# Raw weight slices issued one by one inside the table of orders, on one core

## The chip, the cores and the metric

The kernel runs on one core of a Trainium2 chip. The metric is the device time of one execution in microseconds; the kernel before takes 1088.55 us (median of 3 runs, 1088.54 to 1089.48). The engines are called as in the profile: PE is TensorE's matmul stream, PEld its weight loads, DVE VectorE, ACT ScalarE, POOL GpSimd, SP SyncE. A Q behind the name (ACTq, SPq) marks an instruction that only issues a DMA from that engine's queue.

## The reference

Random-feature attention over 8 batches of 8 heads, 576 tokens, head size 64, 128 features; its output, as a matrix of 4608 tokens by 512, goes through a feed-forward layer of width 2048.

```
def phi(x):                                  # x scaled by 64**-0.25
    proj = einsum('bhsd,md->bhsm', x, omega)
    h = proj - sum(x*x, -1)/2
    h = h - max(h, -1)
    return exp(h) / sqrt(m)
kv  = einsum('bhsm,bhsd->bhmd', phi(k), v);  z = sum(phi(k), axis=2)
num = einsum('bhsm,bhmd->bhsd', phi(q), kv)
den = einsum('bhsm,bhm->bhs', phi(q), z) + 1e-6
x = (num / den) as (tokens, heads*dim)
h = x @ w_in
out = (h - tanh(h)) @ w_out
```

All of it is float32.

## The kernel before

The feed-forward part needs nearly all of TensorE's time. The kernel splits its operands into a hi part (fp32r) and a lo part, and forms each product as hi x hi + hi x lo + lo x hi, three fp32r matmuls in the place of one in float32. Tokens go in 18 chunks of 256, the inner width in 16 slices of 128.

The 16 weight slices arrive as raw 64-bit words, one transfer of 1024 KB each (128 x 1024 words, `raw`), issued from ACT's queue. A slice holds double words of which the kernel makes a float32 by operations on the bits, and then the two fp32r parts. These are the steps of a decoder `d0` to `df`, each a token of the table:

- `is`: issue the raw transfer (ACTq, L619).
- `b` (ACT, L627): the high words to the working buffer `a`; it is the first step that needs the raw slice in place.
- `cl` (POOL, L638; on DVE for d0 and d1): clamp. `v1`, `v2`, `v3` (DVE, L644, L650, L658): shifts and joins of bits.
- `hi` (ACT, L666): the fp32r hi part into the weight's place. `nh` (ACT, L669): minus hi into the lo place.
- `di` (POOL's queue, L672): an accumulating DMA that adds `a` to it, so that the lo part is there when it lands.

The first three batches of keys and the first three chunks of queries are computed by hand-ordered units in float32, at the start. A key unit `kBC` (batch, pair of heads) has `lk` and `lv` (loads on SP's queue, L467, L471), `pj` (projections on PE, L480, L482), `redA`, `redB`, `red5` (minima on DVE, L486, L495), `expA`, `expB`, `exp5` (ACT, L491, L499), `pk0`, `pk1` (products with v on PE, L503, L513), `z` (DVE), `kvf`, `kvwa`, `zb` (ACT copies, L529, L522, L538), `kvwd` (DVE) and `zt` (PE, L533). A query unit `qCC` has `lq` (SP, L551), `pj` (PE, L447), `red` (DVE, L453), `exp` (ACT, L458), `den` (DVE, L562), `nD` and `nA` (DVE and ACT, L569, L574), `pt` (PE transposes, L581), `qt` (ACT, L585), `pn` (PE, L591), `xh` (ACT, L595) and `xl` (DVE). A feed `f0` to `fd` is the feed-forward layer of the first two chunks for one weight slice: `h` (12 matmuls of 512 columns, L373), `th` and `gh` (ACT, L379, L384), `g` and `gl` (DVE, L381, L387), `o` (12 matmuls, L403 to L405). Feed `f0.h` needs all q units of chunks 0 and 1, and each feed needs its own slice's `di` landed.

All these steps stand as 559 tokens in one table, `ORDER`. The program goes through it token by token and every engine and queue gets its instructions in that order, and works through them strictly in it; there is no scheduler in this part. A number behind a step names the buffer or bank it uses (three `kf` and three `v` buffers, two `qf`, eight PSUM banks, three `a` buffers), so a load waits until the buffer's last reader is done. The places of slices 14 and 15 lie over the key buffers, so these two can be issued only when the last key unit has been read. In the table before, the other fourteen `is` tokens are its second to fifteenth.

```
    with tc.manual_schedule():
        for token in ORDER.split():
            name, step_, *slot = token.split(".")
            ...
            units[name][step_](*(int(x) for x in slot))
```

Behind the table come feeds 14 and 15 and then chunks 2 to 17, where a scheduler that goes by modelled times puts the remaining key and query units between the matmuls.

Of the kernel before, what the change touches and what calls it, by code (L numbers as in the profile page):

```python
# [34 lines left out]
TYPES = "dddddddddddddddd"  # L35
BANKS = ("pj0", "pj1", "po0", "po1", "pk", "pt", "h0", "h1")
ORDER = """
k03.lk.0 d0.is d2.is da.is d7.is d4.is d1.is d6.is d3.is dc.is d5.is d9.is d8.is db.is dd.is k01.lk.1 q03.lq.0
k11.lk.2 k03.pj.0.1.2 k01.lv.0 k01.pj.3.4.5 k03.redB k02.lk.0 k03.redA k03.expB.0 k03.red5 q03.pj.6 k01.redB
k12.lk.1 k03.expA.1 k01.red5 q03.red k01.expB.2 k02.lv.1 k01.redA k11.pj.7.1.0 k03.exp5.0 k01.expA.3 k11.lv.2  # L40
k11.redA k01.pk0.4 q03.exp.4 k11.red5 k11.redB k10.lk.2 k11.expA.5 k02.pj.2.3.6 q12.lq.1 k11.exp5.1 k11.expB.6
q13.lq.0 k02.red5 k11.pk0.7 k13.lk.0 k02.redB k02.redA k11.pk1 k02.expB.7 q12.pj.0 k02.expA.3 k11.z k02.pk0.1
k02.exp5.1 q12.red k11.kvf k11.kvwa k02.pk1 k11.kvwd q12.exp.5 k10.lv.2 k11.zt q13.pj.3 k02.z k01.exp5.1
k02.kvf k11.zb k02.zt k12.lv.1 q13.red k01.pk1 k02.zb q12.den q13.exp.6 k13.pj.2.6.0 q01.lq.1 d0.b.0 k01.z
q02.lq.0 q12.nD k03.lv.0 k01.zt q12.nA k13.redB k10.pj.5.7.1 k01.zb k13.redA k13.expB.3 k22.lk.0 k13.red5 d0.cl
q12.pt.3 k13.expA.7 k10.redA q02.pj.6 k23.lk.2 k10.redB k10.expA.2 q01.pj.2 k10.red5 q02.red q00.lq.0
k10.exp5.1 d0.v1 k03.pk0.5 q12.qt.0 q23.lq.1 q02.exp.5 q01.red k03.pk1 d0.v2 k01.kvf q01.exp.1 k10.pk0.1 k03.z
d0.v3 k13.exp5.0 k03.zt k10.expB.0 q12.pn.3 q02.den k10.pk1 k03.zb k00.lv.0 k03.kvf d0.hi q13.den q23.pj.6
k10.kvwa k22.lv.2 k10.kvf d0.nh q00.pj.4 q13.nD k10.z k10.kvwd q13.nA q23.red k12.pj.2.0.7 q11.lq.1 d0.di
d2.b.1 q00.red q21.lq.0 q02.nD k10.zt q23.exp.2 k12.red5 q13.pt.5 k12.redB d2.cl k12.redA q13.qt.1 k12.exp5.1  # L50
q11.pj.6 q03.den k12.expA.0 q13.pn.5 k00.lk.1 k10.zb q11.red q03.nA k12.pk0.7 q03.nD q13.xh q10.lq.1 q01.den
k12.expB.6 q03.pt.2 k12.pk1 q03.qt.0 q01.nD q01.nA q13.xl q03.pn.1 d2.v1 k12.kvwa k12.kvf q00.exp.0 k12.z
k12.kvwd q01.pt.0 d2.v2 k12.zt q21.pj.2 q01.qt.1 k12.zb k23.lv.1 d2.v3 q03.xh q01.pn.5 q02.nA q12.xh q02.pt.4
q03.xl d2.hi q22.lq.0 q12.xl q10.pj.0 q21.red q02.qt.0 k00.pj.7.1.3 q10.red q11.exp.4 q11.den q10.exp.6
q02.pn.4 k00.redB q22.pj.6 q11.nA k00.redA k21.lk.1 q02.xh q01.xh k00.red5 q02.xl k00.expA.1 q01.xl q20.lq.1
q11.nD k00.pk0.0 k00.exp5.1 q22.red d1.b.2 k22.pj.4.5.7 d3.b.0 d1.cl q11.pt.3 d1.v1 k00.expB.5 k22.red5 d3.cl
k22.redB k00.pk1 q11.qt.1 k22.redA k20.lk.0 k22.expB.1 d1.v2 q11.pn.1 k13.lv.0 k00.kvf k22.exp5.1 q20.pj.3
k22.expA.4 k00.z d1.v3 k00.zt k22.pk0.5 q11.xh q20.red k00.zb q22.exp.5 k22.pk1 q11.xl q10.den d1.hi
k21.pj.7.4.0 q10.nD q10.nA q00.den k22.kvwa k13.pk0.1 d1.nh k21.lv.2 k21.redB k13.pk1 q00.nA d1.di k21.red5
k21.expB.4 k21.redA q10.pt.6 k13.z q00.nD k13.zt q10.qt.0 k22.kvwd q00.pt.4 k22.z d3.v1 k13.kvf k13.zb k22.zt  # L60
q00.qt.1 q10.pn.6 q23.den k13.kvwa k21.exp5.1 q00.pn.4 k21.expA.1 k21.pk0.0 q10.xh k13.kvwd q00.xh q23.nD
q23.nA k21.pk1 q00.xl q10.xl k22.zb d3.v2 q21.exp.7 f0.h.7 k20.lv.0 k21.kvwa q21.den d2.nh q20.exp.3 d2.di
k21.z k21.kvwd f1.h.1 d4.b.2 d3.v3 f0.th q21.nD d4.cl d3.hi f0.g q22.den f0.gh q23.pt.4 d3.nh k21.zt
k23.pj.6.5.2 q23.qt.0 f0.gl k21.zb q22.nA q22.nD q23.pn.3 k23.redA f1.th d3.di k23.redB k23.expA.6 q22.pt.7
f1.g k23.pk0.4 q23.xh d4.v1 f1.gh f2.h.0 k23.red5 d6.b.1 f1.gl d4.v2 k23.exp5.0 k23.expB.0 d6.cl d4.v3 q22.qt.1
f0.o f2.th q20.den d4.hi d4.nh f2.g q21.nA f1.o d6.v1 d4.di f2.gh d6.v2 d5.b.0 f2.gl q20.nA d5.cl d6.v3 f3.h.6
q20.nD d6.hi d6.nh f2.o f3.th d6.di f3.g d5.v1 f3.gh d5.v2 d7.b.2 f4.h.7 f3.gl d7.cl d5.v3 d5.hi f3.o f4.th
d5.nh f4.g d7.v1 f4.gh d5.di da.b.1 k23.pk1 f4.gl d7.v2 f4.o k23.kvwa da.cl k23.kvwd k23.z d7.v3 d7.hi k23.zt
q21.pt.0 k23.zb q22.pn.6 d7.nh da.v1 q21.qt.0 f5.h.7 da.v2 d7.di d8.b.0 q22.xh da.v3 d8.cl f6.h.4 da.hi f5.th
da.nh f5.g f5.gh q21.pn.0 da.di f5.gl d8.v1 f7.h.6 f6.th d8.v2 d9.b.2 q21.xh f6.g d9.cl d8.v3 f6.gh f5.o f6.gl  # L70
d8.hi f7.th d8.nh f7.g f6.o d9.v1 f7.gh d8.di dc.b.1 f7.gl d9.v2 dc.cl f7.o d9.v3 d9.hi d9.nh k20.pj.7.0.4
dc.v1 d9.di db.b.0 f8.h.6 k20.redA k20.redB k20.expA.1 db.cl k20.red5 dc.v2 k20.exp5.1 k20.expB.4 k20.pk0.7
dc.v3 f8.th k20.pk1 f8.g dc.hi q20.pt.4 k20.z f8.gh f9.h.0 db.v1 de.is k20.kvwa dd.b.2 f8.gl k20.kvwd db.v2
q20.qt.1 dd.cl df.is dc.nh db.v3 fa.h.6 f9.th f9.g db.hi f9.gh db.nh f8.o f9.gl dc.di dd.v1 fa.th dd.v2 db.di
fa.g f9.o dd.v3 fa.gh fa.gl dd.hi dd.nh fa.o dd.di de.b.1 de.cl k20.zt q20.pn.4 k20.zb df.b.0 fb.h.0 q20.xh
df.cl de.v1 fc.h.6 fb.th de.v2 fb.g de.v3 fb.gh fd.h.7 fb.gl de.hi df.v1 fc.th df.v2 de.nh fb.o fc.g de.di
df.v3 fc.gh fc.gl df.hi fc.o fd.th df.nh fd.g fd.gh df.di fd.gl
"""


# [749 lines left out]
```

## Time and profile before

| | us |
|---|---|
| median of 3 runs | 1088.55 |
| the profiled execution | 1089.21 |
| its span | 1087.2 |
| PE busy (share) | 1046.5 (96%) |
| DVE busy | 804.7 (74%) |
| ACT busy | 677.3 (62%) |
| POOL busy | 278.5 (26%) |
| raw slices: 16 of 1024.0 KB, median to landing | 11.3 |
| `di`: 16 of 512.0 KB, median to landing | 4.8 |
| `k_f`, `v`, `q_f` loads of the table: 288, 320, 128 KB, median to landing | 5.1, 3.6, 3.0 |

The profiled execution is 2.0 us longer than its span, and 0.66 us above the median. Shares of busy time are means over stages that have different limits: PE's 96% holds an opening where it is nearly empty. Matmuls of PE are pipelined and their ends are modelled, so a stretch in which PE counts as busy can hold small gaps; the distance from one start to the next is the better price. Which engine binds is read from a stage's own row.

### The profile page before, as it was taken

To read this page: it belongs to the slowest core of one execution; us is meant where nothing else is said; L and a number is where in the kernel's file an instruction comes from. 1 tells how busy PE (TensorE), PEld (TensorE's weight loads), DVE (VectorE), ACT (ScalarE), POOL (GpSimd) and SP (SyncE) were. 2 spreads that over 40 slices of the span, in tenths; PEclk is the share of its full clock that TensorE was granted. 3 is DMA by queue.
4 is the path that set the end of the run, shared out by engine and by line. 5 is a ranking of instruction groups with operands and counts; after the bars stand their busy time and mean duration, and the time that the engine had idled before them with its cause. 6 is when DMAs were issued, how large, how long until landed. Compare 5 with 4: busy or idle time off the path is not lost.

```text
span 1087.2 us, 20084 instructions
## 1 busy us (share of the span) xinstructions
PE 1046.5 (96%) x6908; PEld 943.9 (87%) x6908; DVE 804.7 (74%) x2761; ACT 677.3 (62%) x1730; POOL 278.5 (26%) x445
## 2 busy tenths in 40 slices
PE   3599999999999999999999999999999999999998
PEld 2577777898999999999999999999999999999997
DVE  1189876677678987688888888999888887666522
ACT  0489766566467665567677767676767675555422
POOL 0012676000123330033333333333333332000000
PEclk7599999999999999999999999999999999999999
DMA  9964447211001110011111111111111110000000
GB/s 365 317 140 96 83 78 182 65 50 34 6 28 52 33 52 11 30 33 52 33 52 33 52 26 39 36 47 33 47 33 52 33 41 11 30 11 26 1 20 20
DMA packets 43462, 64.67 MB, mean 59 GB/s; under 512 B 18656, under 2 KB 28000, under 8 KB 41312
## 3 DMA queue, kind: packets, MB, share of 16 engines
q1 hardware_dynamic: 38672, 38.19, 11.8%
q0 software_dynamic: 2304, 8.39, 4.3%
q10 hardware_dynamic: 2384, 16.81, 3.8%
q8 instruction: 55, 0.90, 0.3%
q14 instruction: 47, 0.39, 0.1%
HBM read 45.55 MB, written 9.44 MB: 51 GB/s over the span
## 4 chain that ended last, share of the span: by engine, by line
PE 79%; DVE 6%; ACT 6%; DMA 5%; issue 2%; POOL 2%; SPq 0%; ACTq 0%; DVEq 0%; POOLq 0%
PE h L373 33%; PE po L403 11%; PE po L404 11%; PE po L405 10%; DMA v<-va 3%; PE pj_q L177 2%; PE pt L325 2%; PE pk L236 2%; PE pn L337 2%; PE pn L336 2%; DVE a L658 1%; ACT k_phi L491 1%; DVE a L650 1%; DMA q_f<-qT 1%; POOL a L638 1%
## 5 line engine op out<-in xcount | busy, mean ns | idle before, releaser
L373 PE MATMUL h<-xh,w 128*128 128x256 f32 (+1 forms) x2176 | 448.2, 291 | 1.2 <-DVE qx L164 0.7
L373 PEld LDWEIGHTS h<-xh,w 128*128 128x128 f32 x2176 | 354.7, 191 | 12.2 <-DMA w<-a 1.3
L373 PE MATMUL h<-xl,w 128*128 128x256 f32 (+1 forms) x1088 | 317.0, 291 | 0.0
L403 PE MATMUL po<-w,gh 128*128 128x512 f32 x544 | 213.9, 393 | 1.3 <-ACT gh L384 1.3
L404 PE MATMUL po<-w,gh 128*128 128x512 f32 x544 | 213.4, 392 | 0.0
L373 PEld LDWEIGHTS h<-xl,w 128*128 128x128 f32 x1088 | 207.8, 191 | 6.0
L405 PE MATMUL po<-w,gl 128*128 128x512 f32 x544 | 211.7, 392 | 0.7 <-DVE gl L387 0.6
L384 ACT CAST gh<-g 128x512 fp32r<-128x512 f32 x144 | 89.4, 621 | 97.7 <-DVE g L381 96.0
L381 DVE TENSOR_TENSOR g<-h,g 128x512 f32<-128x512 f32 x144 | 98.8, 686 | 65.9 <-ACT g L379 64.6
L379 ACT ACTIVATE g<-h 128x512 f32<-128x512 f32 x144 | 85.7, 595 | 98.7 <-PE h L373 92.1
L387 DVE TENSOR_TENSOR gl<-g,gh 128x512 fp32r<-128x512 f32 x144 | 108.4, 753 | 41.0 <-ACT gh L384 39.1
L405 PEld LDWEIGHTS po<-w,gl 128*128 128x128 f32 x544 | 102.2, 188 | 23.9 <-DVE gl L387 3.2
L403 PEld LDWEIGHTS po<-w,gh 128*128 128x128 f32 x544 | 102.5, 188 | 18.6 <-ACT gh L384 2.2
L404 PEld LDWEIGHTS po<-w,gh 128*128 128x128 f32 x544 | 102.5, 188 | 15.6
L185 ACT ACTIVATE phi_q<-phi_q,nb_q 128x128 f32<-128x128 f32 x240 | 78.6, 392 | 2.8 <-DVE nb_q L181 2.5
L220 POOL TENSOR_TENSOR khl<-phi_ka,khl 128x256 fp32r<-128x256 f32 x40 | 31.1, 784 | 179.2 <-DVE khl L219 171.7
L330 DVE TENSOR_TENSOR ql<-pt,qh 128x512 fp32r<-128x512 f32 x60 | 41.2, 686 | 40.5 <-ACT qh L329 40.1
L315 DVE CUSTOM_DVE_ANT_0 junk<-phi_q,zb 128x128 f32<-128x128 f32 (+1 forms) x200 | 60.0, 300 | 11.3 <-ACT phi_q L185 0.3
L638 POOL TENSOR_SCALAR a<-a 128x1024 f32<-128x1024 f32 x14 | 55.3, 3963 | 26.6 <-ACT a L627 25.5
L329 ACT CAST qh<-pt 128x512 fp32r<-128x512 f32 x60 | 34.9, 581 | 42.3 <-PE pt L325 42.0
L181 DVE CUSTOM_DVE_ANT_0 phi_q<-pj_q,phi_q 128x128 f32<-128x128 f32 x240 | 55.6, 283 | 4.1 <-ACT phi_q L178 4.0
L228 POOL CAST vhl<-v 128x128 fp32r<-128x128 f32 (+1 forms) x120 | 37.2, 311 | 79.8 <-PE pk L236 74.5
(158 smaller groups left out, 1850.5 us busy)
## 6 DMA issues: line engine op xcount, KB each, us to landing
raw<-w ACTq DMA_DIRECT2D x16, 1024.0 KB, 11.3
out<-o SPq DMA_DIRECT2D x36, 256.0 KB, 2.0
w<-a POOLq DMA_DIRECT2D x16, 512.0 KB, 4.8
qf<-qT SPq DMA_DIRECT2D x60, 128.0 KB, 2.1
kf<-kT SPq DMA_DIRECT2D x20, 288.0 KB, 2.9
v<-vt SPq DMA_DIRECT2D x20, 288.0 KB, 2.8
v<-va SPq DMA_DIRECT2D x12, 320.0 KB, 3.6
k_f<-kT SPq DMA_DIRECT2D x12, 288.0 KB, 5.1
```

Of the source, the lines that this page charges most:

```text
L181: nc.vector.tensor_tensor_reduce(ph[:, j], pj[:, i, :M], ph[:, j], scale=-SCALE, scalar=3.0e38, op0=ALU.add, op1=ALU.min, accum_out=nb[:, ...
L185: nc.scalar.activation(ph[:, j], ph[:, j], AF.Exp, bias=nb[:, j : j + 1], scale=-1.0)
L315: nc.vector.tensor_tensor_reduce(bank("junk")[r], ph[r, i], kvs[b, c][1][r, h], scale=1.0, scalar=EPS, op0=ALU.mult, op1=ALU.add, accum_ou ...
L373: nc.tensor.matmul(o, w_, x, start=i == 0, stop=i == len(prods) - 1)
L379: nc.scalar.activation(g, p, AF.Tanh)
L381: nc.vector.tensor_sub(g, p, g)
L384: nc.scalar.copy(gh, g)
L387: nc.vector.tensor_sub(gl, g, gh.bitcast(F32))
L403: nc.tensor.matmul(po[t], h, wt[f][:, 0, DM:], start=first, stop=False)
L404: nc.tensor.matmul(po[t], h, wt[f][:, 1, DM:], start=False, stop=False)
L405: nc.tensor.matmul(po[t], l, wt[f][:, 0, DM:], start=False, stop=last)
L638: engine.tensor_scalar(u["af"], u["af"], -TOP, TOP, op0=ALU.max, op1=ALU.min)
```

## The change

Only the string `ORDER` is another. It has the same 559 tokens, in another order and with other buffer and bank numbers, the dependencies being the same. The fourteen `is` tokens that stood in a row at the head now stand one by one between the other steps, the first (`d2.is`) behind 37 tokens, eight ahead of `f0.h` and eight behind it (with `de.is` and `df.is`, which stood there before). Everything else is ordered anew: the first units are q00, q11, k01 and k00 instead of k03, k01, q03 and k11, and the decoders go 2, 5, 0, 1, 3, 4, 7, 6, 8, b, 9, a, c, d, f, e instead of 0, 2, 1, 3, 4, 6, 5, 7, a, 8, 9, c, b, d, e, f. The head of the table:

```
-k03.lk.0 d0.is d2.is da.is d7.is d4.is d1.is d6.is d3.is dc.is d5.is d9.is d8.is db.is dd.is k01.lk.1 q03.lq.0
-k11.lk.2 k03.pj.0.1.2 k01.lv.0 k01.pj.3.4.5 k03.redB k02.lk.0 k03.redA k03.expB.0 k03.red5 q03.pj.6 k01.redB
+q00.lq.0 q11.lq.1 k01.lk.0 k00.lk.1 q00.pj.0 k01.lv.0 q11.pj.1 q00.red k01.pj.2.3.4 q00.exp.0 q11.red q10.lq.0
+q03.lq.1 q11.exp.1 k03.lv.1 k00.pj.5.6.7 k01.red5 k01.redB k01.exp5.0 k01.redA k01.expB.2 k00.lv.2 k00.red5
```

Two places in the engines' own order. First ACT's. Before, the end of its row of raw issues, and the first four things it computes for the attention (names are unit, step and buffer number):

```order
L619 DMA raw_155<-w 128x1024
L619 DMA raw_157<-w 128x1024
L619 DMA raw_159<-w 128x1024
L491 ACTIVATE k_phi_200<-k_pj_168,k_nb_194 128x128 x4
L491 ACTIVATE k_phi_214<-k_pj_167,k_nb_198 128x128 x4
L491 ACTIVATE k_phi_223<-k_pj_182,k_nb_210 128x128 x4
L499 ACTIVATE k_ph_244<-k_pj_169,k_nb_205 128x128
```

After, ACT from its first raw issue (`d2.is`, its twelfth instruction) to the `b` that reads this slice:

```order
L619 DMA raw_252<-w 128x1024
L458 ACTIVATE q_phi_254<-q_pj_219,q_nb_238 128x128 x4
L529 COPY kvf_107<-k_pk 128x128
L499 ACTIVATE k_ph_265<-k_pj_180,k_nb_205 128x128
L491 ACTIVATE k_phi_269<-k_pj_178,k_nb_210 128x128 x4
L458 ACTIVATE q_phi_289<-q_pj_259,q_nb_274 128x128 x4
L538 COPY k_zb<-k_pk 128x256
L491 ACTIVATE k_phi_313<-k_pj_276,k_nb_299 128x128 x4
L574 ACTIVATE q_phi_172<-q_phi_172,q_dn 128x128 x2
L627 ACTIVATE a_331<-raw_252 128x1024
```

All fourteen issues stood ahead of ACT's first exponential; now seven exponential steps stand ahead of the first issue, and eight instructions lie between it and the `b` that needs its data.

Second, the head of SP's queue. Before, the loads of the first units behind the small load of omega:

```order
L467 DMA k_f<-kT 128x576 x2
L551 DMA q_f<-qT 128x256
L467 DMA k_f<-kT 128x576
L471 DMA v_117<-va 128x10x64
L467 DMA k_f<-kT 128x576 x2
L471 DMA v_118<-va 128x10x64
L471 DMA v_119<-va 128x10x64
```

After:

```order
L551 DMA q_f<-qT 128x256 x2
L467 DMA k_f<-kT 128x576 x2
L471 DMA v_117<-va 128x10x64
L551 DMA q_f<-qT 128x256 x2
L471 DMA v_118<-va 128x10x64
L471 DMA v_119<-va 128x10x64
L551 DMA q_f<-qT 128x256
```

Two small q loads have moved ahead of the first k loads, and of the first nine loads four are q's where one was.

More of the change, by code (lines that the diff above doesn't have):

```diff
@@ L37 @@
 ORDER = """
-k03.lk.0 d0.is d2.is da.is d7.is d4.is d1.is d6.is d3.is dc.is d5.is d9.is d8.is db.is dd.is k01.lk.1 q03.lq.0
-k11.lk.2 k03.pj.0.1.2 k01.lv.0 k01.pj.3.4.5 k03.redB k02.lk.0 k03.redA k03.expB.0 k03.red5 q03.pj.6 k01.redB
-k12.lk.1 k03.expA.1 k01.red5 q03.red k01.expB.2 k02.lv.1 k01.redA k11.pj.7.1.0 k03.exp5.0 k01.expA.3 k11.lv.2
-k11.redA k01.pk0.4 q03.exp.4 k11.red5 k11.redB k10.lk.2 k11.expA.5 k02.pj.2.3.6 q12.lq.1 k11.exp5.1 k11.expB.6
-q13.lq.0 k02.red5 k11.pk0.7 k13.lk.0 k02.redB k02.redA k11.pk1 k02.expB.7 q12.pj.0 k02.expA.3 k11.z k02.pk0.1
@@ L43 @@
[L43 to L77, printed above, removed]
+q00.lq.0 q11.lq.1 k01.lk.0 k00.lk.1 q00.pj.0 k01.lv.0 q11.pj.1 q00.red k01.pj.2.3.4 q00.exp.0 q11.red q10.lq.0
@@ new lines @@
+q03.lq.1 q11.exp.1 k03.lv.1 k00.pj.5.6.7 k01.red5 k01.redB k01.exp5.0 k01.redA k01.expB.2 k00.lv.2 k00.red5
+q10.pj.0 k00.redA k01.expA.3 k00.redB q03.pj.1 q02.lq.0 q10.red k00.expB.4 k02.lk.2 k01.pk0.4 q03.red q10.exp.5
+k01.pk1 q21.lq.1 d2.is q03.exp.6 q02.pj.3 k01.z k01.kvf k00.exp5.1 k01.zt k00.expA.7 q02.red k02.pj.2.6.0
+q02.exp.3 k00.pk0.1 k02.redA k11.lv.0 k01.zb q11.den q21.pj.7 k02.expA.2 k03.lk.0 k00.pk1 q11.nD q11.nA
+k02.redB d2.b.0 q11.pt.5 q13.lq.0 k00.z q21.red k00.zt q12.lq.1 k02.red5 k00.zb k20.lk.1 k00.kvf q10.den
@@ new lines @@
+q11.qt.0 d2.cl k02.expB.7 q11.pn.3 k02.lv.2 q10.nD q10.nA k03.pj.4.2.1 q00.den q11.xh k02.exp5.0 k13.lk.2
+q21.exp.4 q00.nD q10.pt.5 q11.xl q13.pj.6 d5.is q10.qt.1 k03.red5 k03.redB q00.nA q10.pn.0 k03.redA k03.expB.1
+q13.red q00.pt.3 k02.pk0.7 d2.v1 q10.xh q00.qt.0 q10.xl k02.pk1 q13.exp.5 d2.v2 q01.lq.0 k03.exp5.1 q00.pn.5
+d0.is d2.v3 k02.kvf k03.expA.0 k13.pj.2.3.0 k02.z q00.xh d2.hi q00.xl k03.pk0.6 k13.red5 d5.b.1 k13.redB k02.zt
+k13.redA k03.pk1 k13.lv.2 k13.exp5.0 k13.expA.2 d5.cl k20.pj.1.4.5 k03.z k10.lv.1 k03.kvf k02.zb k13.expB.7
@@ new lines @@
+q02.den k03.zt q01.pj.0 k11.lk.0 k03.zb d2.nh q03.den k13.pk0.2 q20.lq.0 q02.nA k13.pk1 k12.lk.2 d2.di q13.den
+q03.nA d0.b.2 q12.pj.7 q02.nD q03.nD q13.nA q02.pt.3 k20.redB q03.pt.6 k13.kvwa q02.qt.1 k20.red5 q13.nD
+q03.qt.0 q02.pn.3 k13.z q12.red k20.expB.0 k20.lv.2 k20.redA q03.pn.6 q02.xh d0.cl q12.exp.1 q13.pt.4 q02.xl
+d1.is k13.zt q12.den q20.pj.3 q03.xh k13.zb k20.exp5.1 q13.qt.1 q03.xl q12.nA q20.red k11.pj.7.5.6 k13.kvf
+q12.nD q20.exp.2 q01.red q12.pt.4 k13.kvwd q23.lq.1 q01.exp.7 k11.red5 k11.redA q13.pn.2 db.is q01.den
@@ new lines @@
+k11.exp5.0 q13.xh k12.pj.3.0.6 k11.expA.3 q01.nD k11.redB d1.b.0 k11.pk0.7 q13.xl k12.redA k11.expB.6 q23.pj.2
+k10.lk.1 d1.cl k12.red5 k20.expA.5 k11.pk1 q23.red d4.is k12.redB q23.exp.1 k20.pk0.5 k11.z q23.den k20.pk1
+k11.kvwa k12.exp5.0 k11.kvf q12.qt.0 k11.zt k12.expB.3 q12.pn.1 k20.z k11.kvwd q23.nD k21.lv.0 d0.v1 k11.zb
+k20.zt q12.xh k10.pj.2.6.4 k20.zb q21.den k20.kvwa q23.nA k12.lv.2 q01.nA q23.pt.0 k12.expA.6 q01.pt.7 q21.nD
+k21.lk.0 k20.kvwd q12.xl q21.nA k10.red5 k10.redB q21.pt.5 q23.qt.1 d3.is k10.redA q21.qt.0 q23.pn.3 d0.v2
@@ new lines @@
+k10.expB.5 q21.pn.1 q23.xh d0.v3 k10.expA.0 k21.pj.0.5.6 q21.xh d5.v1 d7.is q01.qt.1 d5.v2 d0.hi k10.pk0.3
+q01.pn.2 k10.exp5.1 k21.redB d0.nh k21.red5 k10.pk1 k21.redA q01.xh k21.expB.1 d5.v3 d0.di k12.pk0.1 k23.lk.2
+k21.exp5.1 k10.z k12.pk1 q01.xl d5.hi d1.v1 d1.v2 k10.kvf d5.nh k10.zt k12.z k10.zb d1.v3 k12.zt k21.expA.7
+d5.di k23.pj.7.4.5 k23.lv.1 q20.den k12.zb k12.kvf d1.hi k21.pk0.6 d1.nh k21.pk1 q20.nD k23.red5 d3.b.2
+k23.redB f0.h.2 d1.di k21.z k23.redA k23.expB.4 d3.cl q20.nA k23.exp5.0 k21.kvwa k23.expA.0 q20.pt.0 k21.kvwd
@@ new lines @@
+k21.zt k23.pk0.4 q20.qt.0 d4.b.1 k22.lk.1 k23.pk1 d3.v1 k21.zb q20.pn.5 d8.is k10.kvwa d3.v2 d4.cl k23.kvwa
+f0.th d7.b.0 f1.h.7 k10.kvwd k23.kvwd k23.z f0.g q20.xh k12.kvwa k12.kvwd f0.gh d3.v3 q22.lq.0 f2.h.0 f0.gl
+d6.is d3.hi d7.cl d4.v1 f1.th d4.v2 d3.nh f1.g k23.zt f0.o d4.v3 f1.gh dc.is k23.zb d3.di f1.gl d4.hi d7.v1
+f2.th d7.v2 f1.o d4.nh f2.g d4.di d7.v3 f2.gh q22.pj.6 f2.gl d7.hi f2.o d7.nh q22.red q22.exp.5 d7.di q22.den
+d6.b.2 f3.h.7 q22.nD q22.nA d6.cl d8.b.1 f4.h.4 da.is f3.th f3.g f3.gh d8.cl d6.v1 f5.h.0 db.b.0 f3.gl d6.v2
@@ new lines @@
+f4.th dd.is f4.g d6.v3 f3.o f4.gh db.cl f4.gl d6.hi d8.v1 d9.is f5.th d8.v2 d6.nh f4.o f5.g d8.v3 f5.gh d6.di
+f5.gl d8.hi q22.pt.6 db.v1 f5.o d8.nh db.v2 q22.qt.1 db.v3 d8.di k22.lv.2 q22.pn.7 db.hi k22.pj.4.0.6 q22.xh
+db.nh f6.h.7 d9.b.2 k22.red5 k22.redB db.di k22.redA k22.exp5.1 k22.expB.6 d9.cl k22.expA.3 f7.h.6 f6.th da.b.1
+f6.g f6.gh da.cl f6.gl f8.h.0 d9.v1 f7.th d9.v2 dc.b.0 f7.g f6.o d9.v3 f7.gh dc.cl f7.gl d9.hi da.v1 f8.th
+da.v2 f7.o d9.nh f8.g da.v3 f8.gh d9.di k22.pk0.4 f8.gl da.hi dc.v1 f8.o da.nh dc.v2 dc.v3 da.di k22.pk1 dc.hi
@@ L78 @@
+dc.nh f9.h.7 k22.z dd.b.2 dc.di df.is k22.kvwa k22.kvwd dd.cl k22.zt f9.th fa.h.6 k22.zb f9.g f9.gh de.is f9.gl
+fb.h.0 dd.v1 fa.th fa.g df.b.1 dd.v2 fa.gh dd.v3 df.cl f9.o fa.gl dd.hi fb.th dd.nh fa.o fb.g fb.gh df.v1 dd.di
+de.b.0 df.v2 fc.h.4 fb.gl de.cl df.v3 df.hi fb.o df.nh fc.th de.v1 df.di fc.g fd.h.7 de.v2 fc.gh fc.gl de.v3
+fc.o fd.th de.hi fd.g fd.gh de.nh fd.gl de.di
 """
```

## The prediction

> **What bounds the kernel now.** I read the page's slices first (40 slices of 27.2 us; tenths of busy time, tenths of TensorE clock), to see where the kernel is not at its steady state.
>
> ```profile
> PE   3599999999999999999999999999999999999998
> PEclk7599999999999999999999999999999999999999
> DMA  9964447211001110011111111111111110000000
> ```
>
> Only the first two slices are off: the DMA engines are full, TensorE is idle or at half clock. From the third slice on TensorE is busy at full clock to the end. So I cut the span by stages: the opening, the attention stage up to the first feed (105.2), the feeds up to the end of the table (199.5, where feed 14 gets the last weights), and the rest. The columns are the stretch, its length, busy us (instructions) of PE, PEld, DVE, ACT, POOL, then granted clock, DMA share, GB/s.
>
> ```profile
> 4.60:61.80 57.20, 28.97 (x174) 24.19 (x176) 11.08 (x32) 15.88 (x57) 0.00 (x0) 0.58 0.89 325
> 61.80:105.20 43.40, 41.84 (x338) 32.77 (x337) 41.19 (x149) 43.40 (x140) 9.37 (x4) 1.00 0.57 129
> 105.20:199.50 94.30, 90.65 (x458) 70.29 (x457) 73.10 (x123) 67.23 (x113) 60.27 (x27) 1.00 0.48 106
> 199.50:1087.20 887.70, 881.49 (x5926) 813.35 (x5926) 678.03 (x2454) 548.85 (x1419) 207.45 (x401) 1.00 0.11 34
> ```
>
> The opening holds 15.88 us of ACT work in 57.2 us. The attention stage is ACT's (43.40 of 43.40), with PE and DVE at 96% and 95%. The feeds and the rest are PE's. Three marks from PE's rows: its first projection, f0.h, and the wait for the last lo half of a decoded weight.
>
> ```profile
> 4.73 1.16 PE L480 MATMUL k_pj<-oms,k_f 64*128 64x128 f32 x16 [0.16 <-DMA k_f<-kT]
> 105.21 0.48 PE L373 MATMUL h<-xh,w 128*128 128x512 f32 x1
> 199.54 0.73 PE L373 MATMUL h<-xh,w 128*128 128x512 f32 x2 [0.49 <-DMA w<-a]
> ```
>
> What empties the opening is seen on ACT's queue and in the waits up to 62 us:
>
> ```profile
> 3.15 31.75 ACTq L619 DMA_DIRECT2D raw<-w  x13
> 34.95 3.20 ACT L491 ACTIVATE k_phi<-k_pj,k_nb 128x128 f32<-128x128 f32 x12 [31.50 <-DMA k_f<-kT]
> ...
> 9.46 15.69 SPq L467 DMA_DIRECT2D k_f<-kT  x2
> ```
>
> ACT issues raw slices until 34.9 and computes nothing, though the first projection of k had started at 4.73. The wait names a load, but the cause is the 13 issues ahead of it in ACT's own queue. SP, which loads q, k and v, has two issues spread over 15.69 us, behind the same burst. The rows of the raw issues follow: all 16 (duration in ns, min/median/max, first and last start), the first four, the fifth, then the time to landing of all 16, and that of the two at 169 to 170 us alone, which had nothing of the burst beside them:
>
> ```profile
> L619 ACTq DMA_DIRECT2D raw<-w x16: 334/335/762, 1.4 to 170.0; - x16
> L619 ACTq DMA_DIRECT2D raw<-w x4: 354/486/762, 1.4 to 4.0; - x4
> L619 ACTq DMA_DIRECT2D raw<-w x1: 334/334/334, 7.8 to 7.8; - x1
> DMA to landing us min/median/max: 6.2/11.3/16.0
> DMA to landing us min/median/max: 6.2/7.1/7.9
> ```
>
> **The change, part by part.** The table holds the same 559 tokens, so no instruction is added or removed; all the gain or loss is in order. (1) Fourteen raw issues leave the head of ACT's queue; eight now stand ahead of f0.h, eight behind it. (2) The loads on SP are put in another order and have no burst of 14 MB beside them. (3) The anneal moves work across f0.h. Counting tokens ahead of f0.h, the new table has one more `b`, one more `hi`, two more `nh`, one `q nA`, two `qt`, two `xh` and two fewer `kvwa` on ACT; on PE one more `k pj`, two more `q pt` and `pn`, one fewer `q pj`.
>
> The sum follows ACT to f0.h, because ACT is what the attention stage is full of, and PE from there.
>
> Start. PE's first projection came at 4.73, just behind its load; the first is now a q projection, which takes 0.96 (80.78 to 81.74 below), and its minimum on DVE 0.69. ACT can start at 4.73 + 0.96 + 0.69 = 6.4.
>
> ```profile
> 14.40 0.69 DVE L453 TENSOR_REDUCE q_nb<-q_pj 128x4 f32<-128x512 f32 x1 [2.79 <-PE q_pj L447]
> ```
>
> ACT's work to f0.h: 15.88 + 43.40 = 59.3 in the old order. The moved instructions are priced by busy us over count in these groups (L627 is `b`, L666 `hi`, L669 `nh`, L574 half an `nA`, L585 `qt`, L595 `xh`, L522 `kvwa`):
>
> ```profile
> L627 ACT ACTIVATE a<-raw 128x1024 f32<-128x1024 f32 x16 | 18.7, 1183 | 0.0
> L669 ACT ACTIVATE w<-a 128x1024 fp32r<-128x1024 f32 x16 | 17.4, 1089 | 0.0
> L666 ACT CAST w<-a 128x1024 fp32r<-128x1024 f32 x16 | 17.4, 1085 | 16.0 <-DVE a L658 16.0
> L574 ACT ACTIVATE q_phi<-q_phi,q_dn 128x128 f32<-128x128 f32 x24 | 9.5, 497 | 0.0
> L585 ACT COPY q_qt<-q_pt 128x512 f32<-128x512 f32 x12 | 7.8, 650 | 0.0
> L595 ACT CAST xh<-q_pn 128x256 fp32r<-128x256 f32 x8 | 3.5, 485 | 0.0
> L522 ACT CAST k_kvw<-k_pk 128x128 fp32r<-128x128 f32 x8 | 2.8, 347 | 0.0
> ```
>
> 1.17 + 1.09 + 2 x 1.09 + 0.79 + 2 x 0.65 + 2 x 0.44 - 2 x 0.35 = 6.7. So 66.0. Raw issues between computing instructions: 8 x 0.335 = 2.7, which nothing hides, since ACT has no idle time there; bounds 0 (they slip into small gaps) and 8 x 0.762 = 6.1; I take 2.7, the median row. The issues behind f0.h fall where ACT is busy 67.23 of 94.3, so they are hidden by its idle time; without that cover they would be 6 x 0.335 = 2.0 more.
>
> Idle time of ACT in the opening (I). With the loads there, ACT of the old kernel was still idle from 34.95 to 61.8 for 26.85 - 15.88 = 11.0 us, because PE fed it at half clock. Bounds: 0 (the attention stage's 43.40 of 43.40) and 11. The clock by three-us stretches (same columns):
>
> ```profile
> 9.00:12.00 3.00, 1.53 (x20) 1.19 (x20) 0.89 (x2) 0.00 (x0) 0.00 (x0) 0.83 1.00 413
> 36.00:39.00 3.00, 2.85 (x19) 2.30 (x20) 0.81 (x2) 3.00 (x14) 0.00 (x0) 0.50 1.14 369
> 57.00:60.00 3.00, 3.00 (x19) 2.50 (x18) 1.65 (x10) 1.39 (x6) 0.00 (x0) 0.70 0.83 191
> 60.00:63.00 3.00, 3.00 (x42) 2.30 (x40) 2.69 (x9) 2.95 (x10) 0.00 (x0) 1.00 0.65 135
> ```
>
> PE was at full clock until about 11, fell to half in a gap, and then stayed there from 36 to 58 though it was busy. The new opening is the same chain of projection, minimum, exponential and product, and its first projections (two q, two k, 2 x 0.96 + 2 x 1.46 = 4.8 us of PE) are over before the first exponentials free the next, so the clock may fall again. But the new stretch is met with the loads landed in order, so I take I = 7, nearer the 11 than the 0. The Trainium skill ("TensorE: Matmul & The Clock Gate", Part 1: The HAM clock gate) has the clock back at full after one busy window of about 3.4 us. By that rule I would be near 2, and the sum 1059; by the rows above, which stay at half through 22 us of busy PE and so disagree with it, 11 and 1068. Any value between keeps the sign.
>
> Waits for raw slices (W). Each `b` on ACT now stands a fixed amount of work behind its own issue, and everything behind it on ACT waits with it: the exponentials, and so PE's products. For d2 these are four runs of four exponentials (12 took 3.20 from 34.95 on, so 4 x 1.07), an `nA` (0.79) and three small copies or exponentials (3 x 0.35, as `kvwa`): 6.1. Counted in the same way the shortest leads ahead of f0.h are about 6 (d2, d1), 7 (d5) and 9 (d0). Against a landing of 6.2 to 7.9 that is 0 to 2 for each of three, 0 to 6 in all; I take 2, since the 6.2 row is a slice alone, as most are now.
>
> So f0.h comes at 6.4 + 66.0 + 2.7 + 7 + 2 = 84.1 instead of 105.2.
>
> The feeds. PE's work moved ahead of f0.h is 1.46 (`k pj`) + 2 x (0.58 + 0.55) (`pn`, `pt`) - 0.96 = 2.8, by the distances between starts here:
>
> ```profile
> 72.12 1.16 PE L480 MATMUL k_pj<-oms,k_f 64*128 64x128 f32 x16
> ...
> 73.58 0.43 PE L533 MATMUL k_pk<-ident,k_z 128*128 128x128 f32 x2
> ...
> 79.38 0.65 PE L591 MATMUL q_pn<-q_qt,kvf 128*64 128x256 f32 x4
> 79.96 0.66 PE L581 MATMUL q_pt<-ident,q_phi 128*128 128x128 f32 x4
> 80.51 0.43 PE L533 MATMUL k_pk<-ident,k_z 128*128 128x128 f32 x2
> 80.78 1.03 PE L447 MATMUL q_pj<-om_bd,q_f 128*128 128x256 f32 x4
> 81.74 0.65 PE L591 MATMUL q_pn<-q_qt,kvf 128*64 128x256 f32 x4
> ```
>
> The stage of 94.3 becomes 91.5, PE still the bound (90.65 of 94.3); the decoders' work on DVE and POOL has 21 and 34 us of slack there. The table ends at 84.1 + 91.5 = 175.6, against 199.5: 23.9 earlier. The rest, 887.7, is PE's and I leave it: the scheduler shifts some rows up to about 300 us, at no cost that I can price (0 to the 6 us that PE idles there).
>
> As a check by PE: the opening's 28.97 busy us of PE at a mean clock of 0.58 are 16.8 at full clock, so 4.7 + 16.8 + 137.7 (61.8 to 199.5) = 159.2 with nothing lost; the same losses of 11.7 give 170.9, 5 below the sum I keep.
>
> The profiled execution took 1089.21 with a span of 1087.2; less 23.9 is 1065.3. The median of the runs is 0.66 below it, so 1064.6, said as 1064.
>
> **Rivals.** (a) The clock is back at once: I is 0 to 2, W is 0, and PE's 3.65 us of idle time between feeds goes too. 1064 - 5 gives 1059, with all three 1051. For it: PE was at full clock until 11 us, and the new start leaves fewer gaps. Against it: the 22 us at half clock above.
> (b) The transfers that moved into the feeds (eight raw slices in that stage, six more than before) slow the accumulating DMAs of the decoders, which now run beside no raw slice except at 170. Feeds 3 to 13 each wait 1 to 2 us: 11 to 22 us lost, 1075 to 1086. For it: the stage's DMA share rises from 0.48. Against it: 106 GB/s leaves much room below the 369 and 413 of the opening.
> (c) Slower: the raw slices land as late as the worst row, 16.0, because loads and accumulating DMAs share the engines with them. Place: the eight `b` with leads under 11 us (d2, d5, d1, d0, d6, d9, de, df, some 62 us of lead in all, those behind f0.h counted in PE work). At 16.0 they wait 8 x 16 - 62 = 66 us on ACT: 1064 + 64, about 1128. It decides from a mean landing of about 11 us, where 8 x 11 - 62 = 26 eats the gain. Against it: the late landings belong to four slices in flight (four were issued by 4.0 and the fifth only at 7.8), and now one or two are.
> (d) The change doesn't do what it says: ACT's order could be overridden by a wait that holds all behind it. The order shows the issues spread over rows 12 to 192 of ACT, so nothing speaks for it: 1088.
>
> **Chances.** The forecast's own case (1060 to 1074) 0.55, (a) 0.25, (b) 0.12, (c) 0.05, (d) 0.03. Under 0.2% (2.2 us) this kernel's runs can't be told from no change. Faster is the first three, 0.92; same 0.03; slower 0.05. The range takes most of (a), all of the first and the near part of (b): 1050 to 1079.
>
> **What would show it.** Right: ACT's first exponential near 6 us, not 35; no stretch of 10 us on ACT's queue with nothing but raw issues; f0.h near 84; the last wait for `w<-a` near 176; the stretch behind it still about 888 long. I: the clock by stretches from 5 to 30 us. W: idle time of L627 put down to the raw DMA. Wrong: f0.h on time but the feeds stretched beyond 95 us (b); ACT waiting for raw slices 3 us and more at each `b` (c); or a clock at half up to f0.h, which would make PE's attention work cost double there.

## The result, and the profile after

The new kernel takes 1061.92 us (median of 4 runs, 1060.27 to 1063.78) against 1088.68 of the old one on the same chip, a ratio of 0.9753, 95% interval 0.9736 to 0.977: 26.8 us less, where 24 were forecast. The range of 1050 to 1079 holds it. The profiled execution took 1060.27 with a span of 1058.5. Its slices of the page (26.5 us each):

```profile
PE   9999998999999999999999999999999999999998
PEclk9999999998999999999999999999999999999999
DMA  8998562100011110011111111111101010000000
```

The two empty slices of PE and the half clock at the head are gone. The DMA engines, full over two slices before, are now at eight to nine tenths over four. There are two new dents: PE's busy share in the seventh slice, at 159 to 185 us, and its clock in the tenth, at 238 to 265 us. The stages, cut at the marks that the prediction used (columns as there), and the rows of the marks:

```profile
7.30:73.27 65.97, 60.66 (x544) 48.66 (x543) 57.66 (x209) 65.23 (x207) 10.14 (x6) 1.00 0.92 263
73.27:168.74 95.47, 91.83 (x443) 72.91 (x442) 67.99 (x95) 62.87 (x104) 57.34 (x27) 1.00 0.70 176
168.74:1058.50 889.76, 879.24 (x5902) 811.21 (x5902) 676.35 (x2451) 549.78 (x1417) 207.53 (x398) 0.99 0.11 33
```

```profile
7.30 2.18 ACT L458 ACTIVATE q_phi<-q_pj,q_nb 128x128 f32<-128x128 f32 x8 [3.04 <-DVE q_nb L453]
...
12.59 0.35 ACTq L619 DMA_DIRECT2D raw<-w  x1
...
73.27 0.48 PE L373 MATMUL h<-xh,w 128*128 128x512 f32 x1
...
168.74 0.73 PE L373 MATMUL h<-xh,w 128*128 128x512 f32 x2 [0.42 <-DMA w<-a]
```

ACT's first exponential comes at 7.3 instead of 35, f0.h at 73.3 instead of 105.2, 31.9 earlier. ACT is busy 65.23 of the 65.97 us between. The end of the span is only 28.7 earlier, so some of it is given back later. Where is seen in the stores of the finished chunks, whose place in the work is the same in both kernels; first the old kernel's (the first two chunks, chunk 2, chunk 3), then the new one's:

```profile
215.52 0.35 SPq L418 DMA_DIRECT2D out<-o  x1
...
265.02 3.37 SPq L418 DMA_DIRECT2D out<-o  x2
...
326.76 3.48 SPq L418 DMA_DIRECT2D out<-o  x2
```

```profile
184.47 8.77 SPq L418 DMA_DIRECT2D out<-o  x4
...
233.00 3.83 SPq L418 DMA_DIRECT2D out<-o  x2
...
297.09 0.34 SPq L418 DMA_DIRECT2D out<-o  x1
```

The lead is 31.1 at the first store, 32.0 at chunk 2's, 29.7 at chunk 3's, and it ends at 28.7.

### The profile page after: what moved, and what is told of

Same layout as the page of the kernel before. It is cut to its first block, busy times and chain, and to the rows that moved or that the text cites. A ratio compares the mean times of both kernels' runs of the same rounds, so it can differ in the third digit from the quotient of the medians.

```text
span 1058.5 us, 20071 instructions
## 1 busy us (share of the span) xinstructions
PE 1038.0 (98%) x6908; PEld 938.4 (89%) x6908; DVE 804.0 (76%) x2761; ACT 679.8 (64%) x1730; POOL 276.4 (26%) x445
## 3 DMA queue, kind: packets, MB, share of 16 engines
q1 hardware_dynamic: 38672, 38.19, 12.1%
## 4 chain that ended last, share of the span: by engine, by line
PE 82%; DVE 7%; ACT 4%; issue 3%; DMA 2%; POOL 1%; DVEq 0%; ACTq 0%; POOLq 0%; SPq 0%
PE h L373 34%; PE po L403 11%; PE po L404 11%; PE po L405 11%; PE pj_q L177 3%; PE pt L325 2%; PE pk L236 2%; DMA w<-a 2%; PE pn L337 2%; PE pn L336 2%; DVE a L650 1%; ACT k_phi L491 1%; DVE a L658 1%; PE pj_ka L177 1%; PE pj_kb L177 1%
## 5 line engine op out<-in xcount | busy, mean ns | idle before, releaser
L315 DVE CUSTOM_DVE_ANT_0 junk<-phi_q,zb 128x128 f32<-128x128 f32 (+1 forms) x200 | 59.9, 300 | 11.3 <-ACT phi_q L185 0.3
L241 POOL TENSOR_TENSOR zt<-phi_ka 128x256 f32<-128x256 f32 x20 | 16.9, 846 | 184.6 <-ACT phi_ka L185 184.6
L638 POOL TENSOR_SCALAR a<-a 128x1024 f32<-128x1024 f32 x14 | 53.1, 3799 | 32.1 <-ACT a L627 32.0
```

Of the source, the lines that this page charges most:

```text
L315: nc.vector.tensor_tensor_reduce(bank("junk")[r], ph[r, i], kvs[b, c][1][r, h], scale=1.0, scalar=EPS, op0=ALU.mult, op1=ALU.add, accum_ou ...
L638: engine.tensor_scalar(u["af"], u["af"], -TOP, TOP, op0=ALU.max, op1=ALU.min)
```

## The experiments

Every experiment is an edit of the old or the new kernel. Where the table was printed anew it takes two lines less, so that code lines there are two lower (the feed's matmul is L371, the raw issue L617).

**Which part earns it: the spread issues or the new order.** The old table with spread issues, and the new table with its issues back at the head:

```
before_spread:  - k03.lk.0 d0.is d2.is da.is ... dd.is k01.lk.1 ...
                + k03.lk.0 k01.lk.1 ... k03.exp5.0 d0.is k01.expA.3 ... q12.pt.3 d2.is k13.expA.7 ...
after_head:     - q00.lq.0 q11.lq.1 ... q02.lq.0 ... d2.is ...
                + q00.lq.0 d2.is d5.is d0.is ... (all fourteen) q11.lq.1 ...
```

> The old table, with each of its fourteen raw issues taken from the head and put about 10 us of ACT work ahead of its own decoder's first step; nothing else moves. Theory A (the burst of issues was the loss, the new anneal adds little): first exponential near 6 us, f0.h at 73 to 80 instead of 105.2, and 1058 to 1066 us in all. Theory B (the new order of units earns a good part): f0.h at 85 or later, 1072 or more.

> The new table, with its fourteen raw issues put back to the head behind the first load; nothing else moves. Theory A: the opening empties again, first exponential near 35 us, f0.h at 100 or later, 1082 to 1095. Theory B: the new order keeps half of the gain, 1075 or less.

Measured: before_spread 1063.86 us, ratio 0.9771 (0.9749 to 0.9793), which can't be told from the new kernel; after_head 1096.42, ratio 1.0072 (1.0047 to 1.0096), slower than the old kernel. In before_spread f0.h stands at 80.42. In after_head ACT's queue does nothing from 3.2 to 30.7 but raw issues, and f0.h is at 108.78:

```profile
3.22 27.43 ACTq L617 DMA_DIRECT2D raw<-w  x13
30.70 2.18 ACT L456 ACTIVATE q_phi<-q_pj,q_nb 128x128 f32<-128x128 f32 x8 [27.19 <-issue]
```

Theory A holds on the total: nearly all of the gain of this kernel is the spread of the issues, and without it the new order loses. Two of its numbers were just missed, f0.h at 73 to 80 in before_spread and at most 1095 us in after_head. The new order brings f0.h 4 to 7 us earlier than the old one with spread issues (73.27 to 76.54 in the profiles with this opening), and has lost that again by the end. The last experiment below shows where.

**What hurts in the burst: the queue that stands still, or the transfers.** The old table as it was, with the fourteen issues on POOL's queue:

```
-            nc.scalar.dma_start(u["raw"], w[f])
+            (nc.gpsimd if f < NW else nc.scalar).dma_start(u["raw"], w[f])
```

> The old table, with the fourteen raw issues still at the head but on POOL's queue, which has nothing else to do there; ACT is free. Theory C (what hurts is ACT's queue standing still behind the issues): first exponential near 7 us, f0.h 20 us or more earlier, 1070 or less. Theory D (what hurts is 14 MB ahead of the loads in the DMA engines): the first v and q loads still land at 25 to 50 us, f0.h at most 8 us earlier, 1080 to 1090.

Measured: 1088.79 us, ratio 1.0007 (0.9998 to 1.0017). ACT is free and starts at 7.6, yet f0.h comes at 104.98. In the next four views stand ACT's first exponentials, its longest wait up to 62 us, the time to landing of the v loads issued up to 36 us, and SP's issues of the second and third of these loads:

```profile
7.61 3.21 ACT L491 ACTIVATE k_phi<-k_pj,k_nb 128x128 f32<-128x128 f32 x12 [4.24 <-DVE k_nb L486]
```

```profile
ACT k_phi L491 <- DVE k_nb L486: 32.4, 4, 26.2
```

```profile
DMA to landing us min/median/max: 30.3/31.3/33.3
```

```profile
16.38 26.60 SPq L471 DMA_DIRECT2D v<-va  x2
```

Theory D holds: to free ACT's blocked queue, which the old profile names as 31.5 us of waiting, gains nothing alone. With it free, ACT waits 26.2 us in one piece further down the chain, because the v loads land after 30 us. The old kernel's own rows agree: its first v load, issued at 4.6, took 28.5 us to land, so it came at 33.1, just ahead of the end of ACT's row of issues at 34.9. So the transfers ahead of the loads hold up the start at least as long as ACT's queue does. Two things stay open. From POOL's queue the burst has another form (a raw slice takes 20.9 us to landing in the median, against 11.3), and no run held ACT's queue without the transfers.

**How close an issue may stand to its use.** The new table with each issue right in front of its `b`:

```
- ... d2.is ... d2.b.0 ... d5.is ... d5.b.1 ...
+ ... d2.is d2.b.0 ... d5.is d5.b.1 ...
```

> The new table with each of the first fourteen raw issues right in front of its decoder's first step, so that ACT stands still for the whole landing. If each landing is 5 to 6 us and ACT waits it out where it binds (four or five ahead of f0.h), and partly behind: f0.h 25 us later (near 98), 40 to 70 us more in all (1100 to 1130). If the landings are hidden by work elsewhere: under 1080.

Measured: 1127.34 us in one run. ACT's waits over the first 250 us, and the raw slices' time to landing:

```profile
ACT a L625 <- DMA raw<-w: 65.5, 14, 7.4
```

```profile
DMA to landing us min/median/max: 4.7/5.8/9.9
```

f0.h is at 95.56, 22 us later, and 18.8 us of the waits stand ahead of it. In all, 65.5 us of waits go with 65 more in the total. That each us of wait costs one is not shown: PE's granted clock is also down, to 0.83 from f0.h to 150 us and 0.81 from there to 210. The loss is of the size of rival (c) of the prediction, with leads of nothing in the place of late landings. The new kernel avoids it, since in its profile ACT waits for no raw slice at all.

**The clock at the start.** One warm-up matmul instead of eight (`for _ in range(1)`), once with the new table, once with the two key projections and their loads moved ahead of the two query projections:

> The new kernel with one warm-up matmul instead of eight, so that TensorE meets its first projections at half clock. If half clock persists for some 20 us of busy matmuls, as in the old kernel from 36 to 58 us: clock 0.5 until 20 us or later, f0.h 5 us or more later, 1066 or more. If a few us of busy matmuls bring it back: clock 1.0 from about 9 us, 1061 to 1064.

> The new kernel with one warm-up matmul and the two key projections (64 rows) ahead of the two query projections (128 rows, 256 columns). If any busy matmuls raise the clock: the key projections' second run is at full clock, 1.16 us per 16. If matmuls that use half of the array don't: both runs take 2.07 as at half clock, and the clock rises only behind the query projections.

Measured: after_cold 1060.71 us (ratio 0.975, 0.9734 to 0.9767), no slower than the new kernel, f0.h at 76.69; after_cold_k 1064.58 in one run. The total of after_cold says little of the clock, since its order at chunk 3 is another (see below). The first rows are PE's projections in after_cold, the next three those of after_cold_k, the last is a stretch of after_cold_k with its clock:

```profile
4.26 3.38 PE L447 MATMUL q_pj<-om_bd,q_f 128*128 128x256 f32 x8 [2.42 <-DMA q_f<-qT]
7.57 1.16 PE L480 MATMUL k_pj<-oms,k_f 64*128 64x128 f32 x16
...
10.49 1.99 PE L447 MATMUL q_pj<-om_bd,q_f 128*128 128x256 f32 x8
```

```profile
4.87 2.08 PE L478 MATMUL k_pj<-oms,k_f 64*128 64x128 f32 x16 [3.03 <-DMA k_f<-kT]
7.50 2.08 PE L478 MATMUL k_pj<-oms,k_f 64*128 64x128 f32 x16
10.12 2.09 PE L445 MATMUL q_pj<-om_bd,q_f 128*128 128x256 f32 x8
```

```profile
6.00:9.00 3.00, 3.00 (x28) 2.44 (x27) 0.00 (x0) 0.00 (x0) 0.00 (x0) 1.00 0.41 95
```

A cold start costs a few us of matmuls at half speed: both key projections at 2.08 instead of 1.16, and the next eight query matmuls at 2.09, near the 1.99 that eight take at full clock in after_cold. So here about 5 us of busy PE bring the clock up, even when the matmuls use 64 rows. Neither half of the expectation came as worded: the second key projection was not at full clock, and the clock rose ahead of the query projections, not behind them. In after_cold, where the query projections come first, it took at most 3.3 us (4.26 to 7.57); one run of each can't say whether the rows make the difference. That agrees roughly with the Trainium skill ("TensorE: Matmul & The Clock Gate", Part 1: The HAM clock gate), which says 3.4 us. Half clock once fallen behind a gap lasted longer, though; this is before_spread, first its gap at a late v load, then three stretches behind it, with the clock third from the end of each row:

```profile
16.33 3.65 PE L501 MATMUL k_pk<-v,k_phi 128*128 128x66 f32 x16 [3.20 <-DMA v<-va]
```

```profile
15.00:18.00 3.00, 1.67 (x8) 1.71 (x9) 0.00 (x0) 1.61 (x7) 0.00 (x0) 0.50 1.00 299
24.00:27.00 3.00, 3.00 (x14) 2.91 (x14) 0.16 (x1) 0.99 (x4) 0.00 (x0) 0.50 0.00 0
27.00:30.00 3.00, 3.00 (x21) 2.50 (x22) 1.67 (x10) 1.40 (x6) 0.00 (x0) 0.78 0.79 197
```

PE is busy from 16.3 on and stays at half until about 28, 12 us. There the rule does not hold. Most of the work in that stretch is products with 66 columns; that these keep the clock down is only argued, no run tested it.

**Whether one early raw slice makes that gap.** before_spread with `d0.is` moved from 8 us behind `k11.pk1`:

```
- ... k03.exp5.0 d0.is k01.expA.3 ...
+ ... k02.redA k11.pk1 d0.is k02.expB.7 ...
```

> The old table with spread issues once more, but the first raw issue, d0, stands behind k11's product instead of 8 us into the kernel, where it ran beside the v loads that the product waited for. If this one slice delays a load, and the 3.2 us gap on TensorE then costs the half clock from 15 to 28 us: clock 1.0 throughout, f0.h at 73 to 77 instead of 80.4, and 3 to 6 us less in all. If the gap and the clock come from the old order of units: as before, f0.h near 80.

Measured: 1062.7 us (ratio 0.9764, 0.974 to 0.9788), f0.h at 79.83. The time is as in the expectation's second case. The wait for v is gone, but the next one takes its place, and the clock falls all the same. The first row is PE's, the second the time to landing of the q loads issued at 11.6 and 12.1:

```profile
18.52 2.03 PE L445 MATMUL q_pj<-om_bd,q_f 128*128 128x256 f32 x4 [1.88 <-DMA q_f<-qT]
```

```profile
DMA to landing us min/median/max: 6.8/7.2/7.6
```

But the edit moved the raw issue only from 8.03 to 11.85 us, and there it runs beside these q loads, which landed in 4.8 to 5.0 us in before_spread. So this run does not part the slice from the old order: one early raw slice may make the gap in both, by another load each time, and no run left it out of the opening. What is shown is that the new order bears such a slice: its first one is issued at 12.59, PE waits for no load from there to f0.h, and the clock stays at 1.00.

**Where the rest was given back.** In the new kernel ACT stands still behind the end of the table. The rows are ACT's, then PE's, then all of PE's longer waits from 168.7 to 241:

```profile
169.27 0.41 ACT L349 CAST xh<-x 128x256 fp32r<-128x256 f32 x1 [5.15 <-PE h L373]
...
171.99 0.59 ACT L379 ACTIVATE g<-h 128x512 f32<-128x512 f32 x1
...
174.05 0.58 PE L373 MATMUL h<-xh,w 128*128 128x256 f32 x1 [2.49 <-DVE g L381]
```

```profile
PE h L373 <- DVE g L381: 2.5, 1, 2.5
PE pj_q L177 <- DVE qx L164: 1.3, 1, 1.3
PE pt L325 <- ACT phi_q L185: 0.9, 1, 0.9
PE h L373 <- ACT xh L349: 0.8, 1, 0.8
```

The new table decodes slice 15 before slice 14, so PE does feed 15 first. ACT's next instruction is a copy of chunk 2 into `xh`, which must wait until feed 14 has read the old `xh`, and feed 14 waits for its weights. Feed 15's tanh, ready at 165, stands behind it in ACT's queue until 172, and PE, which needs that bank for chunk 2, stops for 2.5 us. Exchanging the names of the two decoders in the table makes the order natural:

```
- ... df.is ... de.is ... df.b.1 ... de.b.0 ... fd.gl de.di
+ ... de.is ... df.is ... de.b.1 ... df.b.0 ... fd.gl df.di
```

A second edit starts chunk 3's query units earlier (`[28,30,33,35]` to `[28,29,31,33]`), since their waits make the dent at 238 us; the new kernel ran beside both as the reference.

> The new kernel again, beside the next three on the same chip, as their reference: 1060 to 1064 us.

> The new table with the names of decoders e and f exchanged, so that slice 14 is decoded before slice 15, as the two steps behind the table use them. If the 5 us for which ACT stands behind a copy of x after the table, and PE's 2.5 us wait and clock dip that follow, come from the feeds' exchanged order: those waits go, 2 to 4 us faster than the new kernel. If they are hidden later anyway: within 1 us of it.

> The new kernel with the query units of chunk 3 started at beats 28, 29, 31, 33 instead of 28, 30, 33, 35. If the 3 us given back between the stores of chunks 2 and 3 come from PE waiting for the last of these units: 2 to 3 us faster than the new kernel. If the earlier start takes ACT's and DVE's time from chunk 2: same or slower.

> Both: the gains add up to 4 to 7 us if the two stalls are separate, 1055 to 1058 us.

Measured: after_again 1064.13 us (ratio 0.9767, 0.9745 to 0.9788); after_swap 1052.63 (0.9674, 0.9654 to 0.9694); after_q3 1062.94 (0.9762, 0.9739 to 0.9785); both 1051.5 (0.9667, 0.9649 to 0.9685). The exchange alone is worth 11.5 us, about three times what I expected. The earlier start is worth nothing that can be told, where 2 to 3 us were expected, so the 1055 to 1058 expected for both was missed as well. The same 80 us of the new kernel (first row) and of after_swap (second), and after_swap's stores:

```profile
170.00:250.00 80.00, 73.98 (x463) 67.32 (x462) 56.83 (x211) 48.86 (x119) 0.00 (x0) 0.94 0.11 38
```

```profile
170.00:250.00 80.00, 78.32 (x512) 71.15 (x511) 59.10 (x223) 50.87 (x127) 0.91 (x1) 1.00 0.12 39
```

```profile
180.37 0.35 SPq L416 DMA_DIRECT2D out<-o  x1
...
229.70 3.38 SPq L416 DMA_DIRECT2D out<-o  x2
...
289.96 3.48 SPq L416 DMA_DIRECT2D out<-o  x2
```

PE gains 49 matmuls in that window. 4.3 us are busy time; the mean clock of 0.94 says that 9.6 us of the 80 ran at half, which is another 4.8 us of work. Together they are 9.1, near the 8.3 by which the profiled spans differ (1058.5 to 1050.2; after_again's is 1062.0). So by this estimate half of the loss is the clock that falls behind the stalls. The lead on the old kernel's stores is now 35.2, 35.3 and 36.8.

The exchange of names does two things. From f0.h, which after_swap reaches at 74.35, to the first store it saves 5.2 us (111.2 to 106.0). This is mostly the seam: after_cold, which has the same seam, takes 110.5. From chunk 2's store to chunk 3's it saves another 3.8 (64.1 to 60.3), and there the scheduler's order is another, as PE's rows show, the new kernel's first and then those of after_swap:

```profile
236.42 0.94 PE L177 MATMUL pj_q<-om,qx 128*128 128x256 f32 x4 [1.26 <-DVE qx L164]
...
239.74 0.79 PE L373 MATMUL h<-xh,w 128*128 128x256 f32 x2 [0.79 <-ACT xh L349]
```

```profile
234.17 0.51 PE L371 MATMUL h<-xh,w 128*128 128x256 f32 x2 [0.69 <-DVE qx L162]
234.51 0.68 PE L175 MATMUL pj_q<-om,qx 128*128 128x256 f32 x4
```

In the new kernel four more query projections and their wait stand ahead of chunk 3's first `h`; in after_swap they stand behind it, as in the old kernel. The second stall does not follow from the first: after_cold has the 2.5 us stall at the seam, but after_swap's order at chunk 3, and it too takes 60.3 us between those stores. With both mended, the new order is worth some 10 us more than the old one with spread issues (ratio 0.9674 against 0.9771 of before_spread).

## Why the prediction was right, and which of its steps were not

The direction, the place and the total were right; the total was so partly because two errors of opposite sign cancelled, which is luck. For equal work f0.h came 10.8 us earlier than forecast, the feeds took some 1.4 less, and the rest some 7.5 more: 23.9 forecast and 4.7 on top give 28.6 of the 28.7 by which the spans differ.

- *Start.* 6.4 forecast, 7.3 measured: the first query projections did not yet run at full speed (eight took 2.88 us, where eight take 1.99 later).
- *ACT's work to f0.h.* 66.0 forecast, 65.23 busy measured. This term holds.
- *Raw issues, 2.7.* They cost at most the 0.74 us that ACT was idle in that stage, and with all else that was idle there: an issue runs beside the end of the exponentials before it (the one at 12.59 stands inside a run of exponentials with no idle time marked). My lower bound was the right end.
- *Idle time in the opening, I = 7, and W = 2.* Mis-sized: both together are within the same 0.74. The clock did not fall: it reads 1.00 up to f0.h, where PE's longest wait is 1.1 us. I had carried the old kernel's half clock over to an order that doesn't make its gaps; rival (a) was right on this step. I had also misread that clock: PE was not busy throughout the 22 us from 36 to 58, but waited 2.6 us for a q load at 47.5 (0.88 of 3 us busy from 48 to 51). What stayed at half were two busy stretches of 11 and 8 us, and part of the 11.0 us of ACT's idle time was that wait. Together with the issues it put f0.h at 84.1 where 73.3 was measured (73.3 to 76.7 over the profiles with this opening).
- *The feeds.* 91.5 forecast, 95.5 measured, but the two marks don't enclose equal work: at its last wait for `w<-a` the new kernel has done one more feed's second half and one more feed's first half, 24 matmuls at 0.227 us from start to start. Without these 5.4 us it is 90.1, and the term holds. Rival (b) has nothing in it: the DMA share rose to 0.70, and PE's waits for `w<-a` are 0.4 us.
- *The rest, left as it was.* Failed: 2.1 us longer by the marks although it holds 5.4 us less work, and 8 to 11 us longer than it need be, as after_swap shows. I had seen that the scheduler moves rows there and called it unpriceable between 0 and 6; it lost 7.5. The step that I skipped was to follow ACT's queue past the end of the table with feeds 14 and 15 exchanged; the other part is the scheduler's order at chunk 3.
- *The cause.* I put the empty opening down to ACT's queue first, by the wait row. That was wrong: before_pool shows that to free the queue alone is worth nothing (1088.79 us, f0.h at 104.98), and that with the transfers still at the head the loads come as late.

## What to carry to other kernels

A wait that the profile names can be the first of two in parallel: free the one, and see whether the other ends at the same time, before pricing it. Issue a large transfer some time ahead of its use, but not in a burst ahead of smaller loads that the start depends on and that share the engines. Here leads of 7 us (d2's in the new kernel) to about 10 (before_spread) were enough against landings of about 6; with no lead at all, ACT waited 4.7 us for each. When an order is changed, look at the seam behind it as well: one instruction that waits in an in-order queue there cost 5 us on ACT, 2.5 on PE, and by the clock of 0.83 over the 10 us around it some 1.7 more. And an order found by modelled times can change far behind the edit, so compare the order before a difference is put down to the edit itself.

## What the runs showed of the hardware

The granted clock reads 1.00 from time 0, though the first matmuls run at half speed (2.08 us for 16 where 1.16 is full, at a recorded 1.00): so at the head durations have to be read in its place. The same waits of PE at chunk 3, 1.0 and 0.7 us, are followed by a clock of 0.66 over the next 5 us in the old kernel (270 to 275) and by 1.00 in after_swap and after_cold, so the length of a wait alone does not tell whether the clock falls. With the slices spread a 1 MB transfer lands in 6.3 us (median, the new kernel; 5.8 in after_lead0), where the median was 11.3 with the burst. Moving the issues to another queue did not let the loads past them: the v loads took 31 us to land.
